# Paired-head scores, reordered buffers and engine choices, and 120 identity products in the head of an attention and soft-MoE kernel

## The chip, the cores and the metric

The kernel runs on one core of one Trainium2 chip. The metric is the device time of one execution in microseconds (us), lower is better. Engines: TensorE (PE; PEld is its weight load), VectorE (DVE), ScalarE (ACT), GpSimd (POOL), and SyncE (SP), whose queue issues the DMAs.

## The reference

Three layers follow one another, all in float32. Pooled attention over 8 batches x 8 heads x 576 queries of 64: keys and values are averaged over groups of 8, so each head has 72 of them. Then a dense layer with a rational activation, then a soft mixture of experts with 32 slots.

```python
k_p = k.reshape(B, H, 72, 8, 64).mean(axis=3);  v_p = likewise
attn = softmax(q @ k_p.T / 8);  x = attn @ v_p            # -> x [4608, 512]
h = x @ w_in                                              # [4608, 2048]
P = a0 + a1*h + a2*h**2 + a3*h**3
Q = 1 + |b0|*|h| + |b1|*h**2
x = (P / (Q + 1e-6)) @ w_out                              # [4608, 512]
logits = x @ phi                                          # [4608, 32]
slots = softmax(logits, over tokens).T @ x                # [32, 512]
out_e = relu(slots_e @ w1[e]) @ w2[e]                     # 8 experts, 4 slots each
y = softmax(logits, over slots) @ out                     # [4608, 512]
```

## The kernel before, in words

The 4608 tokens are 36 tiles of 128; four tiles make one of nine runs (r = 0 to 8).

*Head.* K and V of a batch are loaded and summed over the pool (`pooling`, line 323 on: VectorE L330 and L337, or a three-step tree on POOL, L318 to L321). For a tile, `attention` does: scores (PE L364) into two PSUM buffers `sc`, one for even and one for odd heads; maximum and subtraction (DVE L370, L374); exponential (ACT L379); sums and reciprocal (DVE L382, L383); normalization (POOL L389); two transposes (PE L398, ACT L401); the value product (PE L409); and the split into `xh` (ACT L413) and `xl` (DVE L414). The scores of a head take 64 rows: heads 2p and 2p+1 lie on partitions 0 to 63 and 64 to 127 of `q` and `kp`, and each has its own product of 72 columns.

*Weights.* `words` decodes one 128x512 block of `w_in` or `w_out` from 64-bit floats (ACT L427; DVE L428, L430, L432). There are 16 blocks of each. For `w_in`, `win` makes a high and a low part `wh` (ACT L441, POOL L442). For `w_out`, `wout` stores the block to DRAM, transposes it (PE L454) and multiplies it with `phi` (PE L463).

*Runs.* `dense(r, p)` handles one of 8 pairs of `w_in` blocks for the run: 24 products of 512 columns (L484, L485, L486) into a PSUM buffer `h` of 2 x 512, of which there are two; square, affine step and absolute value on ACT (L495, L497, L498); a multiply on POOL (L499); an affine step on DVE (L502); an affine step on POOL (L505); a multiply on POOL (L507); logarithm and exponential on ACT (L510, L513); three steps on DVE (L514, L516, L518); then logits (PE L530), transposes (PE L534) and their copy into `gt` (ACT L543). In run 0 the planner may give L499 and L507 to DVE and L505 to ACT. `routing(r)` ends a run: a running softmax over tokens, and the product `pss` (PE L593) that adds the run to `Sacc`. The attention of run r+1 lies inside run r.

*Tail.* `experts` loads 8 tiles of saved `w_out` and 64 expert tiles of 512 KB each (L628, L634), all from SP's queue in a fixed list, into buffers that come free. `tail` multiplies `Sacc` by `w_out` (PE L654), spreads the slots (L663), runs the two expert layers (PE L708, then PE L737 into `lo2`), finishes the softmax over slots of `cTs` (DVE L750 to L758, PE L765, ACT L768), and then writes the output in 18 steps of 256 tokens: two products into one `h` buffer (PE L788), the first half scaled and copied by ACT (L791), the second by DVE (L793), one store (L795).

*Order.* Nothing is issued in the order of the text. Each step is a task with an engine, a duration from a small table, a key (due time), its tiles, and perhaps alternatives on other engines. `Plan.run` simulates the engines once, on the host, and always takes the task that can start first, ties by key; this fixes each engine's instruction order, the engine of a task with alternatives, and which buffer of a pool a tile gets. At run time each engine executes its list in order. `HEAD`, `FIRST` and `RUN` (30, 105 and 75 us) are the planned lengths of the head, of run 0 and of each later run and set the keys; `LAT` and `SLACK` are the assumed delays from one engine to another and to PE.

```python
k = (round(s, 3), t.key, s + d, t.idx)
if best is None or k < best[0]:
    best = (k, t, i, s)
```

PSUM has eight banks of 512: `h` 2 x 2, `r` 1, `wk` 2, `lg` 1.

Of the kernel before, what the change touches and what calls it, by code (L numbers as in the profile page):

```python
# [18 lines left out]
SP = 72  # L19
# [11 lines left out]

HEAD, FIRST, RUN = 30.0, 105.0, 75.0
# [6 lines left out]
LAT, SLACK = 0.12, 0.6  # L39
# [64 lines left out]
class Task:  # L104
    __slots__ = ("alts", "key", "deps", "outs", "bufs", "n", "end", "start", "idx", "nbytes", "ready", "kind")


class Plan:
# [46 lines left out]
    def run(self):  # L155
# [14 lines left out]
        while left:  # L170
# [66 lines left out]
def soft_moe_kernel(ctx: ExitStack, tc: tile.TileContext, qT, kT, vP, w_in, w_out, ab, phi, w1, w2, sel, pick, out):  # L237
# [11 lines left out]
    for tag, n, w in (("q", 3, 512), ("kv", 3, 1152), ("att", 1, 1024), ("st", 4, 24), ("x", 4, 2048), ("A", 3, 1024),  # L249
                      ("S", 2, 1024), ("U", 3, 1024), ("w", 16, 1024), ("gt", 10, 1024), ("L", 1, 256), ("en", 1, 128), ("m", 3, 4),  # L250
                      ("t", 2, 512), ("wo", 1, 512)):
# [20 lines left out]
    kp = [fixed([128, 4, SP], f"kp{i}", np_=2) for i in range(2)]  # L272
# [12 lines left out]
    den = fixed([128, 1], "den")  # L285
    lgb = buf("lg", [128, 2, 130], "lg", np_=2)
# [7 lines left out]
    op("POOL", 1.0, lambda: make_identity(nc, ident), [], [idb], -100)  # L294
    op("POOL", 0.2, lambda: g_.memset(cc.t, QC), [], [cc], -90)
# [5 lines left out]
    run_len = lambda r: FIRST if r == 0 else RUN  # L301

# [3 lines left out]
    def att_key(t):  # L306
# [3 lines left out]
        if r == 1:  # L310
            return HEAD + 25 + 21.0 * j
# [11 lines left out]
    def pooling(b):  # L323
        need = att_key(first_tile[b])
        for i in range(2):
# [3 lines left out]
            o = kp[b % 2]  # L329
            op("DVE", 1.35, lambda t=t, o=o, i=i: v_.tensor_reduce(out=o.t[:, 2 * i : 2 * i + 2, :], in_=t.t, axis=AX.X, op=ALU.add),  # L330
               [], [t, (o, i)], key, alt=[("POOL", 2.8, lambda t=t, o=o, i=i: tree(t.t, o.t[:, 2 * i : 2 * i + 2, :]), True)] if b != 1 else ())
        for i in range(4):
# [5 lines left out]
               [], [t, (o, i)], key, alt=[("POOL", 2.5, lambda t=t, o=o, i=i: tree(t.t, o.t[:, 128 * i : 128 * i + 128]), True)] if b != 1 else ())  # L338
# [3 lines left out]
    def attention(t):  # L342
# [10 lines left out]
        dma_in(q, lambda: q.t, qT[t], k0 - 30, 128 * 512 * 4)  # L353
# [12 lines left out]
        op("PE", 0.6 * len(sp_), scores, [q] + [kp[x % 2] for x in batches], sc, k0, also=[st, e])  # L366
# [501 lines left out]
```

## Time and profile before

| what | value |
|---|---|
| median of 3 runs | 908.6 us (904.78 to 910.22) |
| the profiled execution | 908.17 us, span 906.4 us |
| mean granted TensorE clock | 0.946 |
| busy: PE, DVE, ACT, POOL | 91%, 69%, 67%, 58% of the span |
| moved by DMA | 97.6 MB, 108 GB/s over the span |

The span runs from the first to the last instruction; the execution's time lies 1.8 us above it. Times in the rows are microseconds from the start of the span unless marked ns. A row of the timeline gives start, length, engine, line, operation, output<-inputs, shapes and count, and in brackets how long the engine had been idle and what released it. Products overlap in TensorE, so their lengths add up to more than the time they take; the distance between their starts is the time that each one costs.

### The profile page before, as it was taken

How to read it: one execution, taken by the hardware profiler on the slowest of the kernel's cores; microseconds unless marked ns; L12 is line 12 of the kernel's file. 1: busy time of each engine (PE TensorE's matmuls, PEld its weight loads, DVE VectorE, ACT ScalarE, POOL GpSimd, SP SyncE). 2: the span in 40 equal slices, each digit the busy share in tenths (PEclk: the TensorE clock that was granted, in tenths of full speed). 3: DMA queues.
4: the chain of work that ended last, by engine and by line, in shares of the span. 5: the costliest groups of instructions: out<-in, count | busy, mean ns of one | idle time of the engine just before them, and what ended most of it. 6: DMA issues, size and time to landing. Idle time of an engine off the chain costs nothing.

```text
span 906.4 us, 15125 instructions
## 1 busy us (share of the span) xinstructions
PE 823.0 (91%) x5950; PEld 582.0 (64%) x5950; DVE 622.7 (69%) x978; ACT 605.9 (67%) x908; POOL 523.5 (58%) x333
## 2 busy tenths in 40 slices
PE   3778859799999999999999999999999999679987
PEld 3567637676777677677677767767777776433321
DVE  5888898946777777867887777758677667631023
ACT  2558757747888787788777868878877787731023
POOL 3225242856777778668866958667676766800000
PEclk9999869789999999999999999999999999869975
DMA  9694332240012100200130111000000443749947
GB/s 315 252 331 130 125 121 96 77 126 13 25 39 71 33 25 27 91 25 13 39 102 12 39 51 56 25 1 25 1 2 1 135 144 107 232 166 357 417 183 278
DMA packets 34151, 97.60 MB, mean 108 GB/s; under 512 B 3872, under 2 KB 4128, under 8 KB 34080
## 3 DMA queue, kind: packets, MB, share of 16 engines
q1 hardware_dynamic: 34080, 96.63, 31.1%
q8 instruction: 47, 0.77, 0.3%
q14 instruction: 24, 0.20, 0.1%
HBM read 82.99 MB, written 13.63 MB: 107 GB/s over the span
## 4 chain that ended last, share of the span: by engine, by line
PE 74%; DVE 12%; ACT 8%; DMA 2%; issue 2%; POOL 1%; SPq 0%; DVEq 0%; ACTq 0%; POOLq 0%
PE h L484 14%; PE h L486 13%; PE h L485 13%; PE gp L534 7%; PE av L409 4%; PE pss L593 4%; PE lg L530 4%; PE pt L398 3%; PE lo L737 3%; PE sc L364 3%; PE po L788 2%; DVE a L502 2%; PE l L708 2%; DVE r L516 2%; DVE u L514 1%
## 5 line engine op out<-in xcount | busy, mean ns | idle before, releaser
L484 PE MATMUL h<-xh,wh 128*128 128x512 f32 x576 | 249.5, 433 | 16.9 <-DVE a L502 8.6
L499 POOL TENSOR_TENSOR a<-a,s 128x1024 f32<-128x1024 f32 (+1 forms) x69 | 163.4, 2369 | 123.3 <-ACT a L497 112.9
L486 PE MATMUL h<-xh,wh 128*128 128x512 f32 x576 | 232.1, 403 | 0.5 <-POOL wh L442 0.3
L485 PE MATMUL h<-xl,wh 128*128 128x512 f32 x576 | 231.3, 402 | 0.0
L514 DVE SCALAR_TENSOR_TENSOR u<-u,r 128x512 f32<-128x512 f32 x144 | 98.2, 682 | 109.0 <-ACT r L513 105.3
L507 POOL TENSOR_TENSOR u<-u,s 128x1024 f32<-128x1024 f32 (+1 forms) x70 | 165.0, 2358 | 6.4 <-ACT s L504 1.2
L484 PEld LDWEIGHTS h<-xh,wh 128*128 128x128 f32 x576 | 111.4, 193 | 45.2 <-DVE a L502 12.3
L486 PEld LDWEIGHTS h<-xh,wh 128*128 128x128 f32 x576 | 111.0, 193 | 28.3 <-POOL wh L442 2.2
L485 PEld LDWEIGHTS h<-xl,wh 128*128 128x128 f32 x576 | 112.0, 195 | 18.1
L543 ACT ACTIVATE gt<-gp 128x512 f32<-128x512 f32 x143 | 79.8, 597 | 49.4 <-PE gp L534 47.9
L516 DVE SCALAR_TENSOR_TENSOR r<-a,abt,r 128x512 f32<-128x512 f32 x144 | 107.9, 749 | 0.0
L502 DVE SCALAR_TENSOR_TENSOR a<-h,abt,a 128x1024 f32<-128x1024 f32 (+1 forms) x73 | 92.2, 1264 | 20.1 <-POOL a L499 19.9
L518 DVE SCALAR_TENSOR_TENSOR a<-u,r 128x512 f32<-128x512 f32 x144 | 98.5, 684 | 4.3
L513 ACT ACTIVATE r<-s 128x512 f32<-128x512 f32 x144 | 86.8, 603 | 20.7 <-DVE a L518 19.8
L505 POOL TENSOR_SCALAR s<-u,gb 128x1024 f32<-128x1024 f32 (+1 forms) x71 | 84.4, 1188 | 16.3 <-DVE a L499 9.8
L498 ACT ACTIVATE u<-h 128x1024 f32<-128x1024 f32 (+1 forms) x73 | 73.7, 1011 | 26.1 <-PE h L486 25.7
L510 ACT ACTIVATE s<-u,cc 128x1024 f32<-128x1024 f32 (+1 forms) x73 | 83.2, 1140 | 6.9 <-POOL u L507 6.7
L497 ACT ACTIVATE a<-h,abt 128x1024 f32<-128x1024 f32 (+1 forms) x73 | 87.3, 1195 | 0.0
L534 PE MATMUL gp<-ident,a 128*128 128x128 f32 x576 | 84.0, 285 | 1.9 <-ACT cTs L587 1.1
L495 ACT ACTIVATE s<-h 128x1024 f32<-128x1024 f32 (+1 forms) x73 | 73.5, 1009 | 17.8 <-PE h L486 17.7
L534 PEld LDWEIGHTS gp<-ident,a 128*128 128x128 f32 x576 | 63.6, 143 | 22.0 <-issue 16.8
L389 POOL TENSOR_TENSOR at<-at,st 128x576 f32<-128x576 f32 x35 | 41.1, 1176 | 33.3 <-DVE st L383 29.7
(123 smaller groups left out, 1060.8 us busy)
## 6 DMA issues: line engine op xcount, KB each, us to landing
wx<-in_w SPq DMA_DIRECT2D x64, 512.0 KB
kst<-in_kT SPq DMA_DIRECT2D x16, 576.0 KB
qt<-in_qT SPq DMA_DIRECT2D x36, 256.0 KB
vst<-in_vP SPq DMA_DIRECT2D x32, 288.0 KB
out_dram<-o SPq DMA_DIRECT2D x18, 512.0 KB
raw<-in_w_in SPq DMA_DIRECT2D x16, 512.0 KB
raw<-in_w_out SPq DMA_DIRECT2D x16, 512.0 KB
wod<-wo SPq DMA_DIRECT2D x16, 256.0 KB
```

What stands on the lines that cost most here:

```text
L484: p_.matmul(o, w[:, 0, k], xh[r].t[:, k], start=(k == 0), stop=False)
L485: p_.matmul(o, w[:, 0, k], xl[r].t[:, k], start=False, stop=False)
L486: p_.matmul(o, w[:, 1, k], xh[r].t[:, k], start=False, stop=(k == 3))
L497: op("ACT", t_act(n, 1, 2), lambda fl=fl: a_.activation(out=fl(A), in_=fl(h), func=AF.Identity, scale=a3, bias=a2), [pt_(h), abt], [pt_(A) ...
L499: mul = lambda eng, fl=fl: eng.tensor_tensor(out=fl(A), in0=fl(A), in1=fl(S_), op=ALU.mult)
L502: op("DVE", t_dve(n, 1), lambda fl=fl: v_.scalar_tensor_tensor(out=fl(A), in0=fl(h), scalar=a1, in1=fl(A), op0=ALU.mult, op1=ALU.add), [pt ...
L507: mul = lambda eng, fl=fl: eng.tensor_tensor(out=fl(U), in0=fl(U), in1=fl(S_), op=ALU.mult)
L513: op("ACT", t_act(512, 0), lambda f=f, q=q: a_.activation(out=q.t, in_=S_.t[:, f], func=AF.Exp, scale=-1.0), [(S_, f)], [q], c + 10)
L514: op("DVE", t_dve(512), lambda f=f, q=q: v_.scalar_tensor_tensor(out=U.t[:, f], in0=U.t[:, f], scalar=QC, in1=q.t, op0=ALU.add, op1=ALU.mult),
L516: op("DVE", t_dve(512, 1), lambda f=f, q=q: v_.scalar_tensor_tensor(out=q.t, in0=A.t[:, f], scalar=a0, in1=q.t, op0=ALU.add, op1=ALU.mult) ...
L518: op("DVE", t_dve(512), lambda f=f, q=q: v_.scalar_tensor_tensor(out=A.t[:, f], in0=U.t[:, f], scalar=-2.0, in1=q.t, op0=ALU.add, op1=ALU. ...
L534: p_.transpose(pt.t[:, j, f, :], A.t[:, f, o : o + 128], ident)
```

## The change

The diff changes seven things.

1. Scores of two heads become one product. `kp` grows to 2 x 72 columns per pair of heads, zero but for two blocks; ACT copies the pooled keys into the blocks. A tile has four products of 128 rows and 144 columns. Heads are now grouped by pair in `sc` and after it.
2. The queries of the first four tiles get keys ahead of the values' loads, and 120 products of the identity with itself, which nothing reads, get the last key (1e6), so the planner puts one wherever TensorE would be idle in its plan, until they are used up. They hold the `lg` buffer until then.
3. The constants of the plan: `HEAD` 27.6, `FIRST` 105.03, keys of run 1's attention, a dense block 1.40 in place of 1.37, `SLACK` 0.86, and no delay for a buffer that was never used.
4. Engine choices (`E0`, `EITHER`, `AD`, `GD`): in run 0 POOL keeps both multiplies (L499, L507); in run 8 the last four pairs may use DVE or ACT for them and for L505, L497 may go to DVE, and the copy of the last two pairs to DVE.
5. In run 8 the last two pairs are handled in halves (before: the last one), and `r` may also use `wk` from pair 4 on.
6. Expert tiles 28 and 29 go into `q` and `at` buffers as halves, and later ones may also use `kv` and `att`. The transposed `w_out` block uses `att` or `gt`; its own buffer is gone.
7. The softmax over slots is normalized in `cTs` by DVE. In the output loop every second step uses an `h` buffer that one engine copies whole (1024 columns, ACT or DVE), the others use two banks of `wk` and `r`, each copied by ACT or DVE.

```diff
-HEAD, FIRST, RUN = 30.0, 105.0, 75.0
+HEAD, FIRST, RUN = 27.6, 105.03, 75.0
+FINE, EITHER = 2, 4
+RW, GD, AD = 4, 6, 0
+A1, A1S = 26.91, 19.0
+FILL = 120
+E0 = 12
-LAT, SLACK = 0.12, 0.6
+LAT, SLACK = 0.12, 0.86
...
-                        s0 = max(s0, c[0] + LAT)
+                        s0 = max(s0, c[0] + LAT if c[0] else 0.0)
...
-    kp = [fixed([128, 4, SP], f"kp{i}", np_=2) for i in range(2)]
+    kp = [fixed([128, 4, 2 * SP], f"kp{i}", np_=2) for i in range(2)]
...
+    idle = buf("lg", [128, 128], "idle")
...
+    for _ in range(FILL):
+        op("PE", 0.22, lambda: p_.matmul(idle.t, ident, ident, start=True, stop=True), [idb], [idle], 1e6)
...
+    for i in range(2):
+        op("POOL", 0.75, lambda i=i: g_.memset(kp[i].t, 0.0), [], [kp[i]], -94)
...
-            return HEAD + 25 + 21.0 * j
+            return HEAD + A1 + A1S * j
...
+            for par in range(2):
+                rr = slice(64 * par, 64 * par + 64)
+                op("ACT", 0.33, lambda o=o, i=i, par=par, rr=rr: a_.activation(out=kp[b % 2].t[rr, 2 * i : 2 * i + 2, SP * par : SP * par + SP], in_=o.t[rr], func=AF.Copy),
+                   [o], [(kp[b % 2], i)], key + 0.1)
...
-        dma_in(q, lambda: q.t, qT[t], k0 - 30, 128 * 512 * 4)
+        dma_in(q, lambda: q.t, qT[t], (k0 if t > 3 else -8.2 + 0.1 * t) - 30, 128 * 512 * 4)
...
-                    for par in range(2):
-                        rr = slice(64 * par, 64 * par + 64)
-                        p_.matmul(sc[par].t[t0:t1, SP * p : SP * p + SP], q.t[rr, p, t0:t1], kp[bb % 2].t[rr, p, :], start=True, stop=True)
+                    p_.matmul(sc[p // 2].t[t0:t1, 2 * SP * (p % 2) : 2 * SP * (p % 2) + 2 * SP], q.t[:, p, t0:t1], kp[bb % 2].t[:, p, :], start=True, stop=True)
...
-        subs = [(0, 1), (1, 2)] if r == NR - 1 and p == NPAIR - 1 else [(0, 2)]
+        subs = [(0, 1), (1, 2)] if r == NR - 1 and p >= NPAIR - FINE else [(0, 2)]
+        either = r == 0 or r == NR - 1 and p >= EITHER
...
-               alt=[("DVE", t_dve(n), lambda mul=mul: mul(v_), True)] if r == 0 else ())
+               alt=[("DVE", t_dve(n), lambda mul=mul: mul(v_), True)] if (E0 & 1 if r == 0 else either) else ())
...
-            q = buf("r", [128, 512], "r")
+            q = buf(["r", "wk"] if r == NR - 1 and p >= RW else "r", [128, 512], "r")
...
+            if 28 <= n < 30:
+                halves = [buf("q", [128, 512], "wx"), buf("q" if n == 28 else "at", [128, 512], "wx")]
...
-                b = buf(["kv", "att"] if n < 8 else ["w", "gt", "A"], [128, 2, 512], "wx")
+                b = buf(["kv", "att"] if n < 8 else ["w", "gt", "A", "kv", "att"], [128, 2, 512], "wx")
...
+            op("DVE", t_dve(n), lambda c3=c3, cm=cm, nt=nt: v_.tensor_tensor(out=c3(), in0=c3(), in1=cm(2).rearrange("p (a o) -> p a o", o=1).to_broadcast([128, nt, 32]), op=ALU.mult),
+               [csum], [cr], kk, port=True)
...
-            po = buf("h", [128, 2, 512], "po", np_=2)
+            po = [buf("h", [128, 2, DM], "po")] if n % 2 == 0 else [buf(["wk", "r"], [128, DM], "po") for _ in range(2)]
...
+            for i in range(len(po)):
+                w = 2 * DM // len(po)
+                oo = lambda i=i, o=o, po=po: o.t if len(po) == 1 else o.t[:, i]
+                op("ACT", t_act(w), lambda i=i, oo=oo, po=po: a_.activation(out=oo(), in_=po[i].t, func=AF.Copy), [po[i]], [o if len(po) == 1 else (o, i)], kk,
+                   alt=[("DVE", t_dve(w), lambda i=i, oo=oo, po=po: v_.tensor_copy(oo(), po[i].t), False)])
```

## Rows read from the trace of the kernel before

**Rows 1.** The page, part 1: busy us, share of the span, instructions.

```profile
PE 823.0 (91%) x5950; PEld 582.0 (64%) x5950; DVE 622.7 (69%) x978; ACT 605.9 (67%) x908; POOL 523.5 (58%) x333
```

**Rows 2.** Stretches: length, busy us of each engine (instructions), granted clock, DMA share, GB/s.

```profile
6.00:55.00 49.00, 30.21 (x204) 23.34 (x205) 41.14 (x71) 20.54 (x34) 15.82 (x15) 1.00 0.87 306
55.00:219.00 164.00, 142.76 (x943) 111.75 (x942) 129.02 (x195) 108.68 (x173) 81.21 (x61) 0.86 0.37 121
219.00:749.00 530.00, 519.99 (x4076) 388.23 (x4079) 394.43 (x624) 417.89 (x609) 390.84 (x228) 1.00 0.14 42
781.00:806.00 25.00, 12.34 (x104) 7.42 (x102) 16.19 (x26) 15.07 (x30) 12.93 (x10) 0.64 0.66 220
806.00:820.00 14.00, 11.83 (x87) 4.90 (x87) 3.11 (x10) 2.50 (x6) 0.29 (x1) 0.90 0.70 269
...
868.00:907.00 39.00, 28.35 (x74) 8.46 (x74) 13.85 (x19) 12.71 (x20) 0.00 (x0) 0.57 0.64 243
```

**Rows 3.** The timeline of TensorE, the head.

```profile
8.20 1.99 PE L364 MATMUL sc<-kp,qt 64*128 64x72 f32 x16 [8.20 <-DMA qt<-in_qT]
14.28 2.10 PE L364 MATMUL sc<-kp,qt 64*128 64x72 f32 x16 [4.09 <-DMA qt<-in_qT]
...
42.43 1.23 PE L364 MATMUL sc<-kp,qt 64*64 64x72 f32 x30 [0.25 <-ACT a L401]
49.62 1.98 PE L409 MATMUL av<-a,vp 72*64 72x128 f32 x16 [5.96 <-DVE at L374]
...
55.06 0.77 PE L484 MATMUL h<-xh,wh 128*128 128x512 f32 x1
...
57.34 0.59 PE L486 MATMUL h<-xh,wh 128*128 128x512 f32 x1
57.76 0.40 PE L484 MATMUL h<-xh,wh 128*128 128x512 f32 x1
57.99 0.39 PE L485 MATMUL h<-xl,wh 128*128 128x512 f32 x1
```

**Rows 4.** The chain that ended last: start, us, what; ends of run 0 and run 7.

```profile
219.12 3.57 PE pss L593 x32
...
748.57 3.57 PE pss L593 x32
```

**Rows 5.** The timeline of TensorE at the scores of a tile in run 1.

```profile
241.03 1.12 PE L364 MATMUL sc<-kp,qt 64*128 64x72 f32 x16
242.07 0.50 PE L484 MATMUL h<-xh,wh 128*128 128x512 f32 x1
```

**Rows 6.** The timeline of POOL in the drain.

```profile
780.67 2.39 POOL L499 TENSOR_TENSOR a<-a,s 128x1024 f32<-128x1024 f32 x1 [3.34 <-ACT s L495]
...
791.62 2.50 POOL L507 TENSOR_TENSOR u<-u,s 128x512 f32<-128x512 f32 x2
```

**Rows 7.** Groups of the whole span: count | busy us, mean ns | idle before.

```profile
L587 ACT ACTIVATE cTs<-ptr 128x128 f32<-128x128 f32 x9 | 2.5, 277 | 0.0
```

**Rows 8.** The timeline of TensorE, one pair's transposes in run 8.

```profile
765.50 1.09 PE L534 MATMUL gp<-ident,a 128*128 128x128 f32 x8
```

**Rows 9.** Groups of VectorE from 55 to 220 us.

```profile
L499 DVE TENSOR_TENSOR a<-a,s 128x1024 f32<-128x1024 f32 x4 | 5.0, 1249 | 5.6 <-ACT a L497 5.6
...
L507 DVE TENSOR_TENSOR u<-u,s 128x1024 f32<-128x1024 f32 x3 | 3.7, 1219 | 0.0
```

**Rows 10.** Stretches of the expert weights, columns as in rows 2.

```profile
810.00:864.00 54.00, 51.02 (x330) 18.75 (x323) 4.75 (x9) 4.68 (x9) 0.29 (x1) 1.00 0.96 379
850.00:860.00 10.00, 10.00 (x33) 2.86 (x32) 0.00 (x0) 0.00 (x0) 0.00 (x0) 1.00 1.03 419
```

**Rows 11.** The output loop: TensorE's timeline, then VectorE's group from 868 us on.

```profile
894.17 3.34 PE L788 MATMUL po<-so,cTs 32*128 32x512 f32 x8 [0.31 <-DVE o L793]
897.82 2.48 PE L788 MATMUL po<-so,cTs 32*128 32x512 f32 x6 [0.31 <-DVE o L793]
...
L793 DVE TENSOR_SCALAR o<-po,csum 128x512 f32<-128x512 f32 x18 | 13.4, 750 | 19.1 <-ACT o L791 19.1
```

More of the change, by code (lines that the diff above doesn't have):

```diff
@@ L104 @@
 class Task:
-    __slots__ = ("alts", "key", "deps", "outs", "bufs", "n", "end", "start", "idx", "nbytes", "ready", "kind")
+    __slots__ = ("alts", "key", "deps", "outs", "bufs", "n", "end", "start", "idx", "nbytes", "ready", "kind", "name")
 class Plan:
@@ L328, in pooling @@
             dma_in(t, lambda t=t: t.t, kT[b, i], key - 30, 128 * 2 * SP * 32)
[L329 to L331 removed]
+            o = buf("ks", [128, 2, SP], "ks")
+            op("DVE", 1.35, lambda t=t, o=o: v_.tensor_reduce(out=o.t, in_=t.t, axis=AX.X, op=ALU.add),
+               [], [t, o], key, alt=[("POOL", 2.8, lambda t=t, o=o: tree(t.t, o.t), True)] if b > 1 or b == 0 and E0 & 8 else ())
+            for par in range(2):
+                rr = slice(64 * par, 64 * par + 64)
+                op("ACT", 0.33, lambda o=o, i=i, par=par, rr=rr: a_.activation(out=kp[b % 2].t[rr, 2 * i : 2 * i + 2, SP * par : SP * par + SP], in_=o.t[rr], func=AF.Copy),
+                   [o], [(kp[b % 2], i)], key + 0.1)
         for i in range(4):
@@ L337, in pooling @@
             op("DVE", 1.2, lambda t=t, o=o, i=i: v_.tensor_reduce(out=o.t[:, 128 * i : 128 * i + 128], in_=t.t, axis=AX.X, op=ALU.add),
-               [], [t, (o, i)], key, alt=[("POOL", 2.5, lambda t=t, o=o, i=i: tree(t.t, o.t[:, 128 * i : 128 * i + 128]), True)] if b != 1 else ())
+               [], [t, (o, i)], key, alt=[("POOL", 2.5, lambda t=t, o=o, i=i: tree(t.t, o.t[:, 128 * i : 128 * i + 128]), True)] if b > 1 or b == 0 and E0 & 8 else ())
     xh, xl = {}, {}
@@ L361, in scores @@
                 for t0, t1, bb in sp_:
-                    for par in range(2):
-                        rr = slice(64 * par, 64 * par + 64)
-                        p_.matmul(sc[par].t[t0:t1, SP * p : SP * p + SP], q.t[rr, p, t0:t1], kp[bb % 2].t[rr, p, :], start=True, stop=True)
-        op("PE", 0.6 * len(sp_), scores, [q] + [kp[x % 2] for x in batches], sc, k0, also=[st, e])
+                    p_.matmul(sc[p // 2].t[t0:t1, 2 * SP * (p % 2) : 2 * SP * (p % 2) + 2 * SP], q.t[:, p, t0:t1], kp[bb % 2].t[:, p, :], start=True, stop=True)
+        op("PE", 1.0 + 0.2 * (len(sp_) - 1), scores, [q] + [kp[x % 2] for x in batches], sc, k0, also=[st, e])
         v3 = lambda par: sc[par].t[:, 0 : 4 * SP].rearrange("p (h s) -> p h s", s=SP)
@@ L486, in g1 @@
                         p_.matmul(o, w[:, 1, k], xh[r].t[:, k], start=False, stop=(k == 3))
-                seq("g1", op("PE", 1.37, g1, [wh[2 * p + f], xh[r], xl[r]], [(h, f)], c - step + f * step / 2, after=was("g1"), kind="g"))
+                seq("g1", op("PE", 1.40, g1, [wh[2 * p + f], xh[r], xl[r]], [(h, f)], c - step + f * step / 2, after=was("g1"), kind="g"))
         A, S_, U = (buf(x, [128, 2, 512], x.lower(), np_=2) for x in "ASU")
-        subs = [(0, 1), (1, 2)] if r == NR - 1 and p == NPAIR - 1 else [(0, 2)]
+        subs = [(0, 1), (1, 2)] if r == NR - 1 and p >= NPAIR - FINE else [(0, 2)]
+        either = r == 0 or r == NR - 1 and p >= EITHER
         for f0, f1 in subs:
@@ L496, in dense @@
             seq("sq", P.tasks[-1])
-            op("ACT", t_act(n, 1, 2), lambda fl=fl: a_.activation(out=fl(A), in_=fl(h), func=AF.Identity, scale=a3, bias=a2), [pt_(h), abt], [pt_(A)], c)
+            op("ACT", t_act(n, 1, 2), lambda fl=fl: a_.activation(out=fl(A), in_=fl(h), func=AF.Identity, scale=a3, bias=a2), [pt_(h), abt], [pt_(A)], c,
+               alt=[("DVE", t_dve(n, 1), lambda fl=fl: v_.tensor_scalar(out=fl(A), in0=fl(h), scalar1=a3, scalar2=a2, op0=ALU.mult, op1=ALU.add), False)] if r == NR - 1 and p >= AD else ())
             op("ACT", t_act(n), lambda fl=fl: a_.activation(out=fl(U), in_=fl(h), func=AF.Abs), [pt_(h)], [pt_(U)], c)
@@ L615, in experts @@
             key += 0.01
+            if 28 <= n < 30:
+                halves = [buf("q", [128, 512], "wx"), buf("q" if n == 28 else "at", [128, 512], "wx")]
+                w, e, k = it
+                v = lambda b: b.t if len(b.t.shape) == 2 else b.t.rearrange("p a h s -> p (a h s)")[:, 0:512]
+                for h, b in enumerate(halves):
+                    src = (w1 if w == 1 else w2)[e, k][:, 512 * h : 512 * h + 512]
+                    op("SP", 0.06, lambda b=b, src=src, v=v: nc.sync.dma_start(out=v(b), in_=src), [], [b], key, nbytes=128 * 2048)
+                ew[it] = (halves, lambda h, halves=halves, v=v: v(halves[h]))
+                continue
             if n < 4 or 24 <= n < 28:
@@ L632, in experts @@
                 o = lambda b=b, at=at: at(b)
-                ew[it] = ((b, part), o)
+                ew[it] = ([(b, part)], lambda h, o=o: o()[:, h])
                 op("SP", 0.06, lambda o=o, src=src: nc.sync.dma_start(out=o(), in_=src), [], [(b, part)], key, nbytes=128 * 4096)
```

31 lines of the change are left out of this document (14 added, 17 removed).

## The prediction

> **What bounds the kernel now.** I read the page first: TensorE busy 91% of the span, VectorE 69% [rows 1]. Busy shares hide stages, so the stretches come next [rows 2]. The reader should see five of them.
>
> - From 6 to 55 us TensorE is busy 30.2 of 49 us, VectorE 41.1. Nothing is close to its limit, so this is a chain. In the order of TensorE [rows 3] the first scores start at 8.20, the second tile's wait 4.09 us for its queries, the fourth tile's value product waits 5.96 us for VectorE, and the first dense product is at 55.06. Equal dense products stand 0.42 us apart there and 0.23 us apart from 57.76 on, 2.7 us into back-to-back work: the spacing goes from that of 1.2 GHz to that of 2.4, although the clock column says 1.00 for the whole stretch.
> - From 55 to 219 us (run 0, ended by its routing product at 219.12, [rows 4]) VectorE is busy 129 of 164 us, because it also decodes the weights; TensorE 143, part of it at half clock (granted 0.86).
> - From 219 to 749 us, seven runs take (748.57 - 219.12)/7 = 75.6 us each with TensorE busy 520 of 530 us. That is bound by TensorE; all waiting there is 10 us.
> - From the last dense product to the last routing product (781 to 806) TensorE is idle half the time: the last pairs drain through POOL, VectorE and ScalarE.
> - From 806 on DMA bounds the expert weights, and the output loop follows from 870.
>
> **The change part by part.**
>
> *Paired scores.* Per tile, eight 64-row products of 72 columns become four 128-row ones of 144; each fp32 product is two instructions. Before: 16 instructions from 241.03 to the next product at 242.07, 0.065 us each for 72 columns [rows 5]. Twice the columns at twice the time, half as many: 1.04 us again, 0 over the 36 tiles. Bounds: 0.041 us per instruction, as in the form with 64x64 blocks [rows 3], is 0.7 us and thus 0.4 us gained per tile, -13 us; the same 0.4 us lost is +13. I take 0, from the row of the same row count.
> The Trainium skill, "TensorE: Matmul & The Clock Gate", Part 3, says that products of few rows in different row groups run side by side; by it the change undoes a packing that was worth half of the old 1.04 us, and the sum would be 36 x 0.5 = 18 us worse. The spacing of 0.065 us in the old one-batch form shows no such overlap.
> The zero padding is two memsets of 128x576 on POOL. They stand in the 8.2 us in which TensorE waits for its first data [rows 3], and even at the 2.4 us of a POOL pass over 128x1024 [rows 6] both end by then; 0. Placing the two halves costs ScalarE 32 copies of about 0.28 us [rows 7], 9 us over the kernel; ScalarE is busy 418 of 530 us in the steady part, which hides them; in the head the last two sit in front of the first scores: +0.6 us.
>
> *Query order and the 120 products.* All four query tiles now precede the values in SP's queue. The second scores lose their wait: 4.09 us, of which about 2 are due anyway, since the two score buffers of the first tile come free only after their VectorE steps (I put half of the wait down to these). The values land some 2 us later; nothing shown waits for them in that part. The filler products: one 128x128 fp32 product is two instructions. At full clock eight such instructions took 1.09 us [rows 8], so at most 0.27 us a product; at half clock I scale that by the dense products, 0.42/0.23 [rows 3], to 0.50. For 120 that is 33 or 60 us. TensorE is idle 19 of the 49 us [rows 2] and all of the 6 before, and at full clock its own 30 us shrink to 15, leaving 40. The products start when the identity is ready (an estimate: 1.4 us, after two short POOL steps); if the clock rises as it did at 57.76, some 3 us go at half speed, and 33 + 3 + 15 = 51 fits into 55 and they stand in idle time. What they can cost is queue position: TensorE executes in order, so scores that become ready early stand behind them. What they bring: the eight scores, transposes and value products per tile at 2.4 GHz. Scores took 1.99 us in the head against 1.04, so about 3 us per tile with the others, on a chain that passes two PSUM buffers in turn. Four tiles: -12 us at best for the chain. But VectorE must still decode all weights; what it wins is its idle time before 55 us, at most 8 us (49 us of window, 41.1 busy, [rows 2]). Bounds: -8 and, at half clock, +36 (below). I take -4, half of that idle time.
>
> *Run 0.* The multiplies may no longer go to VectorE: 4 + 3 of them, 5.0 + 3.7 = 8.7 us [rows 9], move to POOL at 2.39 us each, 16.7 us [rows 6]; POOL is busy 81 of 164 us, so there is room. VectorE, busy 129 of 164 us, has the most to lose there after TensorE, so I credit 8.7 us, less 1.7 for the longer latency: -7. Bounds: 0 if run 0 is held by the chain through POOL, -20 if the half-clock stretches go too. If the longer POOL chain is fully exposed: +8 (7 x 1.14). New keys for run 1's attention only reorder.
>
> *Runs 1 to 7.* No work removed. A longer assumed latency can save part of 10 us of waits: -1, between +3 and -6.
>
> *Drain.* POOL does the multiplies of the last pairs in series, one starting at 780.67 and the last two halves from 791.62 to 794.12 [rows 6], 13 us after the last dense product; VectorE's steps and the transposes follow. With halves for the last two pairs, and VectorE or ScalarE allowed to take multiplies and affine steps, VectorE's 1.25 us (or about 0.7 per half) replaces 2.4. VectorE is idle 8.8 of 25 us there, ScalarE 10. Moving three POOL multiplies of 2.4 saves about 7 us of POOL's queue and adds 3.7 to VectorE: I take -5, between -2 and -8. Next in line is the three-step VectorE chain per half.
>
> *Expert weights.* From 810 to 864 DMA moved 20.5 MB; at the 419 GB/s of 850 to 860 that is 49 us of 54 [rows 10]. The products of the second layer cannot end before the last tile, so the transfer bounds 867. Two tiles of 0.52 MB now go early into query and attention buffers: -2.5 us. Four more buffers, free when the products of the linear layer end, can fill part of the other 5 us, in which it waited for buffers: I credit 2. Together -4.5, between -2 and -7. The earlier drain shifts this transfer by its own 5 us, since the buffers it waits for are freed by the last routing product.
>
> *Output.* Each of 18 steps is a product, a ScalarE copy, then a VectorE copy; VectorE waits 19.1 us for ScalarE in total, and one buffer's circle (product, copy, copy) takes 3.65 us for every second step: TensorE's rows of the same buffers stand 3.65 us apart [rows 11]. The clock fell to a granted mean of 0.57 there while TensorE waited [rows 2]. With one reader per buffer and 7 banks in place of 4, two steps cost VectorE at most 2 x 0.75 us [rows 11] for its halves, while ScalarE takes the 1024-wide one: under 0.8 us a step. Then DMA bounds: 18 x 0.524 = 9.44 MB at 380 GB/s (243 at a share of 0.64 over the stretch, [rows 2]) is 24.8 us. With an estimated 2.5 us ahead of the first store (one product, one wide copy) and as much after the last one, the loop takes 29.8 us from 870, where it took 36.4: -6.5, between -4 and -9. The normalization moves into three VectorE steps; like the subtractions beside them they lie between 806 and 820, where all of VectorE's work is 3.1 of 14 us [rows 2]: 0.
>
> Sum: -4 + 0.6 - 7 - 1 - 5 - 4.5 - 6.5 = -27.4. The profiled execution took 908.2 us (span 906.4), 0.4 below the median of 908.6. So 880.8, I say **881**.
>
> **The rivals.**
>
> 1. *Run 0 keeps its time.* VectorE's gain is used up by POOL's longer chain, and what the head wins is waited out at the weights. For it: TensorE is busy 143 of run 0's 164 us too. Against: VectorE is the fullest engine there. Only steady part, drain, weights and output are left: -17, so 891.
> 2. *Run 0 gains more.* Better packed, TensorE keeps 2.4 GHz: the granted 0.86 over 164 us with 143 busy means about 20 us lost to half clock. Getting most of it: 881 - 18 = 863.
> 3. *The products block the head (slower).* If the clock falls back between them because each real step still waits for data, 60 us of products plus 30 of work end at 91 instead of 55: +36. Run 0 has 164 - 143 = 21 us of idle to catch up; with half of it +26, and less the tail's 16 about 918; without catching up 928. It decides from the point at which the head and run 0 lose over 16 us, the tail's sum. Against: in [rows 3] it rose 2.7 us into dense work.
> 4. *Pairing costs TensorE time.* A loss of 0.5 us for each of 36 tiles in a part bound by TensorE: 881 + 18 = 899. For it: the 0.041 us spacing of one form; against: 0.065 in the form used by 32 tiles.
> 5. *The order gets worse.* The planner's order is new everywhere, and its table gives run 0 105 us where the trace has 164: 15 to 25 us lost somewhere in runs 0 to 7: 896 to 906.
>
> **How the numbers follow.** Forecast 0.45, rival 1 0.22, rival 2 0.17, rival 3 0.05, rival 4 0.04, rival 5 0.07. A measurement of this kernel tells about 1%, 9 us. Faster by over 1% (below 899.5): the forecast, rivals 1 and 2, and a good third of 4 and 5: 0.88. Within 1%: the rest of 4 and 5: 0.07. Slower: 0.05. The range takes in the forecast, rival 1 with its spread, and most of rival 2: 862 to 898.
>
> **What would show it.** Right: scores at about 1 us per tile with 8 instructions; filler products at 0.21 to 0.27 us apart from some 4 us on; first dense product at 45 to 52; first routing product at 205 to 212; 75 to 76 us per run after it; last dense to last routing product 19 to 21 us instead of 25; two weight tiles before the gap; output loop of 27 to 30 us with DMA share near 1 and no ScalarE-to-VectorE wait in it. Wrong: filler products at 0.43 us or more all along, a first dense product after 60, run 0 ending after 219, or an output loop that still takes 34 us.

## The result, and the profile after

The changed kernel takes 877.2 us (median of 4 runs, 875.8 to 882.4) where the kernel before takes 906.7 beside it (904.4 to 910.2): a ratio of 0.968, interval 0.963 to 0.974. Forecast were 881 us and a range of 862 to 898. The profiled execution took 878.2 us, its span 876.4. The total is right; run 0's term and the pairing's are not, and their errors cancel in part.

The kernel after, the page, part 1 (columns as in [rows 1]):

```profile
PE 810.1 (92%) x5870; PEld 597.6 (68%) x5870; DVE 622.6 (71%) x976; ACT 613.3 (70%) x941; POOL 534.5 (61%) x336
```

VectorE is as busy as before to a tenth of a microsecond. So the 30 us are not work taken from it. Next the stretches of the kernel after, in the columns of [rows 2]; the borders follow its own stages, which end earlier:

```profile
6.00:48.00 42.00, 40.09 (x375) 38.24 (x375) 34.94 (x62) 20.64 (x40) 13.26 (x13) 1.00 0.95 332
48.00:211.00 163.00, 139.18 (x899) 111.37 (x899) 135.26 (x204) 118.14 (x190) 91.57 (x55) 0.91 0.40 128
211.00:736.00 525.00, 517.13 (x3852) 392.13 (x3850) 395.44 (x625) 418.88 (x625) 396.94 (x237) 1.00 0.14 44
768.00:788.00 20.00, 11.36 (x87) 6.80 (x90) 12.85 (x24) 11.39 (x24) 7.76 (x7) 0.67 0.69 264
788.00:844.00 56.00, 53.34 (x359) 19.09 (x355) 6.25 (x15) 5.28 (x11) 0.29 (x1) 0.96 0.87 347
844.00:877.00 33.00, 13.79 (x74) 3.91 (x74) 6.65 (x10) 14.49 (x20) 0.00 (x0) 0.75 0.76 286
```

From 6 to 48 us TensorE is now busy 40 of 42 us, but much of that is filler. VectorE's 34.9 of 42 and DMA's share of 0.95 (0.87 from 6 to 55 us in [rows 2]) are the ones that do work. The chain that ended last has the routing products, whose starts in [rows 4] were 219.12 and 748.57:

```profile
211.29 3.60 PE pss L609 x32
...
736.37 3.57 PE pss L609 x32
787.84 5.79 PE pss L609 x32
```

With the first dense product (48.22, shown below; 55.06 in [rows 3]) and the first output product (846.52; 870.18 before) these give the table. Before, run 8's routing product started at 806.00.

| stage | before | after | difference |
|---|---|---|---|
| start to first dense product | 55.06 | 48.22 | -6.8 |
| to the routing product of run 0 | 164.06 | 163.07 | -1.0 |
| runs 1 to 7 | 529.45 | 525.08 | -4.4 |
| run 8, with the drain | 57.43 | 51.47 | -6.0 |
| routing to first output product | 64.2 | 58.7 | -5.5 |
| output loop | 36.2 | 29.9 | -6.3 |
| sum | 906.4 | 876.4 | -30.0 |

The head, TensorE's timeline of the kernel after (columns as in [rows 3]):

```profile
1.36 10.31 PE L303 MATMUL idle<-ident 128*128 128x128 f32 x66 [1.36 <-POOL at L307]
11.51 1.15 PE L378 MATMUL sc<-kp,qt 128*128 128x144 f32 x8
...
44.81 1.09 PE L423 MATMUL av<-a,vp 72*64 72x128 f32 x16 [1.23 <-DVE at L388]
48.22 0.77 PE L498 MATMUL h<-xh,wh 128*128 128x512 f32 x1
...
51.36 0.41 PE L499 MATMUL h<-xl,wh 128*128 128x512 f32 x1
51.60 0.39 PE L500 MATMUL h<-xh,wh 128*128 128x512 f32 x1
```

Three things are to be seen. The first row is 33 products in one piece (a product is two instructions); the scores behind them start at 11.51, though ScalarE has placed the second half of their keys by 8.53: it starts that copy at 7.88 and takes 0.65. The waits of 4.09 us for the queries and of 5.96 us for VectorE [rows 3] are gone, the latter down to 1.23. And the dense products still begin at half speed: 0.24 us apart only from 51.36 on, 3.1 us into them. The granted clock of 48 to 51 us, 0.50, says it too:

```profile
48.00:51.00 3.00, 3.00 (x10) 2.42 (x10) 2.93 (x6) 1.54 (x4) 1.30 (x1) 0.50 0.63 178
```

The output loop of the kernel after, groups of the stretch from 840 us on, against 19.1 us in which VectorE waited for ScalarE [rows 11]:

```profile
L822 ACT ACTIVATE o<-po 128x1024 f32<-128x1024 f32 (+1 forms) x18 | 13.7, 808 | 4.8 <-PE po L816 4.8
L823 DVE COPY o<-po 128x512 f32<-128x512 f32 x9 | 6.2, 692 | 10.2 <-PE po L816 10.2
```

Both readers now wait for TensorE alone.

### The profile page after: what moved, and what is told of

The parts are those of the page before. It is cut to its first block, busy times and chain, and to the rows that moved or that the text cites. A ratio compares the mean times of both kernels' runs of the same rounds, so it can differ in the third digit from the quotient of the medians.

```text
span 876.4 us, 15025 instructions
## 1 busy us (share of the span) xinstructions
PE 810.1 (92%) x5870; PEld 597.6 (68%) x5870; DVE 622.6 (71%) x976; ACT 613.3 (70%) x941; POOL 534.5 (61%) x336
## 4 chain that ended last, share of the span: by engine, by line
PE 76%; DVE 9%; ACT 8%; issue 2%; POOL 2%; DMA 1%; SPq 0%; ACTq 0%; DVEq 0%; POOLq 0%
PE h L498 14%; PE h L500 13%; PE h L499 13%; PE gp L550 7%; PE pss L609 4%; PE av L423 4%; PE lg L546 4%; PE idle L303 3%; PE pt L412 3%; PE sc L378 3%; PE lo L762 3%; DVE a L518 2%; PE l L733 2%; PE po L816 1%; DVE r L532 1%
## 5 line engine op out<-in xcount | busy, mean ns | idle before, releaser
L515 POOL TENSOR_TENSOR a<-a,s 128x1024 f32<-128x1024 f32 (+1 forms) x73 | 171.7, 2352 | 127.1 <-ACT a L512 105.1
L499 PE MATMUL h<-xl,wh 128*128 128x512 f32 x576 | 230.8, 401 | 0.0
L523 POOL TENSOR_TENSOR u<-u,s 128x1024 f32<-128x1024 f32 (+1 forms) x74 | 173.0, 2339 | 7.9 <-ACT s L520 2.6
L499 PEld LDWEIGHTS h<-xl,wh 128*128 128x128 f32 x576 | 111.4, 193 | 17.9
L518 DVE SCALAR_TENSOR_TENSOR a<-h,abt,a 128x1024 f32<-128x1024 f32 (+1 forms) x74 | 92.3, 1247 | 8.3 <-POOL a L515 7.5
L521 POOL TENSOR_SCALAR s<-u,gb 128x1024 f32<-128x1024 f32 (+1 forms) x67 | 79.4, 1186 | 9.6 <-DVE a L515 2.9
L512 ACT ACTIVATE a<-h,abt 128x1024 f32<-128x1024 f32 (+1 forms) x66 | 78.8, 1193 | 0.0
```

Source lines behind the costliest of these rows:

```text
L499: p_.matmul(o, w[:, 0, k], xl[r].t[:, k], start=False, stop=False)
L515: mul = lambda eng, fl=fl: eng.tensor_tensor(out=fl(A), in0=fl(A), in1=fl(S_), op=ALU.mult)
L518: op("DVE", t_dve(n, 1), lambda fl=fl: v_.scalar_tensor_tensor(out=fl(A), in0=fl(h), scalar=a1, in1=fl(A), op0=ALU.mult, op1=ALU.add), [pt ...
L523: mul = lambda eng, fl=fl: eng.tensor_tensor(out=fl(U), in0=fl(U), in1=fl(S_), op=ALU.mult)
```

## The experiments

Each is the changed kernel with one edit, unless said. Executions of the same kernel spread by up to 8.5 us, so stages are compared as well as medians.

**The products not issued.** The 120 tasks stay in the plan, so every other instruction keeps its place, but nothing is executed for them.

```diff
-op("PE", 0.22, lambda: p_.matmul(idle.t, ident, ident, start=True, stop=True), [idb], [idle], 1e6)
+op("PE", 0.22, lambda: None, [idb], [idle], 1e6)
```

> The 120 identity products stay in the plan, so that every engine keeps its order, but are not issued. Theory A (they earn the earlier dense start by raising TensorE's clock in the head): scores back to about 2 us per tile, first dense product at 53 to 56 us instead of 48.2, the whole 5 to 8 us longer, 882 to 885. Theory B (the earlier start comes from the query order and the new order alone, and the products only stand in front of the first scores): first scores at 8.6 instead of 11.5, first dense product at 45 to 48, the whole 873 to 877.

880.4 us (875.3 to 883.8), ratio 0.971 (0.967 to 0.976). TensorE's timeline of this run:

```profile
6.81 1.30 PE L378 MATMUL sc<-kp,qt 128*128 128x144 f32 x4 [6.81 <-ACT kp L346]
...
43.11 1.98 PE L423 MATMUL av<-a,vp 72*64 72x128 f32 x16 [1.72 <-DVE at L388]
...
48.55 0.77 PE L498 MATMUL h<-xh,wh 128*128 128x512 f32 x1
```

and its stretch of the head:

```profile
6.00:48.00 42.00, 27.77 (x154) 21.49 (x154) 35.33 (x63) 21.19 (x41) 13.32 (x13) 0.73 0.92 333
```

The first half of the scores starts 4.7 us earlier (the second at 8.80), TensorE has a granted clock of 0.73 in place of 1.00, and the first dense product is at 48.55 in place of 48.22. What stays equal is VectorE's work (35.3 us) and the rate of the loads (333 GB/s).

The equal end of the head hides two differences. One is when VectorE comes to its fourth sum of a value block (L353), first in the kernel after, then in this run:

```profile
38.12 1.22 DVE L353 TENSOR_REDUCE vp<-vst 72x128 f32<-72x1024 f32 x1 [0.40 <-DMA vst<-in_vP]
```

```profile
36.61 1.22 DVE L353 TENSOR_REDUCE vp<-vst 72x128 f32<-72x1024 f32 x1 [0.58 <-DMA vst<-in_vP]
```

It is 1.5 us earlier here, and the last value product before the dense part follows it (43.11 against 44.81). The other is the clock: from this value product to the first dense product it is 5.4 us here, at a granted clock of 0.50 (1.2 GHz), and 3.4 us in the kernel after, at 0.96. So the clock is worth 2.0 us in this place, and the earlier sum made up for it.

**The first 24 products priced at half clock,** so that the plan puts fewer of them ahead of the scores.

```diff
-for _ in range(FILL):
-    op("PE", 0.22, ...
+for i in range(FILL):
+    op("PE", 0.34 if i < 24 else 0.22, ...
```

> The plan prices the first 24 products at 0.34 us instead of 0.22, so 22 instead of 33 stand in front of the first scores; the other engines keep their order. If the 3 us that the first scores wait behind products are on the path to the first dense product: first scores at about 8.6, first dense product 2 to 3 us earlier, 874 to 875. If the head is set by what comes after (value loads, VectorE, the two score buffers): first scores earlier, the rest as it was, 877.

878.5 us (875.0 to 880.2). The scores start at 8.83, 2.7 us earlier; the first dense product is at 48.42. The delay of the first scores costs nothing that shows: VectorE, now earlier too, waits 1.93 us for the load of its fourth sum and starts it at 38.37. Of the products 14 now stand at 41.82, behind the last scores (one in the changed kernel), and the dense products begin at full speed here (0.33 us apart, then 0.23); run 0 is not shorter for it (165.2 us).

**200 products.**

```diff
-FILL = 120
+FILL = 200
```

> 200 products in place of 120, so that the plan fills TensorE past 43 us, where the products end and the clock falls before the dense part. If the clock at the dense start matters: first dense products at full clock, about 1.5 us gained, 875 to 876. If the products cost their place in TensorE's queue: each of the 80 more takes 0.18 us and up to 14 us are lost, 880 to 891.

885.8 us (884.3 to 888.8), some 7 us above the run before, on the same chip. TensorE's timeline:

```profile
43.24 3.39 PE L303 MATMUL idle<-ident 128*128 128x128 f32 x28
...
50.95 0.48 PE L498 MATMUL h<-xh,wh 128*128 128x512 f32 x1
51.26 0.39 PE L499 MATMUL h<-xl,wh 128*128 128x512 f32 x1
```

The dense products begin at full speed (0.31 us apart; 0.42 and more in the changed kernel), as they did in the run before, and start 2.5 us later than there; run 0's routing product is at 217.46. Of the 5.9 us between the two profiles 2.5 lie in the head, 1.3 in run 0 and 2.6 in runs 1 to 7. The missing warm start was not the loss. A product takes 0.22 us at the full clock in the kernel after (18 of them 4.01 us from 15.93 on), where 0.18 was expected.

**Run 0's multiplies free again to go to VectorE.**

```diff
-E0 = 12
+E0 = 15
```

> In run 0 VectorE may take the multiplies again, as before the change. By the step of the prediction (VectorE is what run 0 waits for, 8.7 us of multiplies cost 7 us): run 0 gets 5 to 7 us longer, 882 to 884. By the rival read from the trace after (VectorE's total up to the end of run 0 did not change, because value reductions took the place of the multiplies): run 0 within 3 us of 163, the whole within 4 us of 877.

885.2 us (884.1 to 887.3): 4.8 above the first run and 6.7 above the second, all on one chip, with no overlap of the runs. VectorE has the multiplies again (4 at L515, 3 at L523, 9.1 us). By these medians the step is worth some 5 to 7 us. The profile does not put them where they were forecast: run 0 takes 167.2 us, against 166.5 and 165.2 in the first two runs, and the head ends 1.7 and 1.8 us later than theirs. VectorE's total to the end of run 0 is 175.8 us here, against 171.5 and 171.4, so the choice by itself does relieve VectorE. But in the change as a whole that total did not fall: 170.5 us in 219 before, 171.6 in 211 after. Two groups of VectorE tell why, first the kernel before, from 0 to 219 us:

```profile
L337 DVE TENSOR_REDUCE vp<-vst 72x128 f32<-72x1024 f32 x8 | 9.6, 1205 | 3.5 <-DMA vst<-in_vP 3.5
L428 DVE TENSOR_SCALAR wi<-wi 128x512 int32<-128x512 int32 x16 | 6.7, 419 | 0.0
```

and the kernel after, from 0 to 211:

```profile
L353 DVE TENSOR_REDUCE vp<-vst 72x128 f32<-72x1024 f32 x13 | 15.6, 1207 | 2.9 <-DMA vst<-in_vP 2.9
L442 DVE TENSOR_SCALAR wi<-wi 128x512 int32<-128x512 int32 x16 | 9.7, 606 | 0.1
```

Five sums of values came over from POOL, 6.0 us. The 16 decode steps of this group take 606 ns on average instead of 419, 3.0 us more, but all decode steps together (L442, L444 and L446; L428, L430 and L432 before) only 66.1 us instead of 64.6, since another group became shorter.

**Scores unpaired, everything else changed.** The keys stay in the wide buffer; eight products of 64 rows and 72 columns read its blocks, and the value product takes the heads in the old order.

```diff
-p_.matmul(sc[p // 2].t[t0:t1, ...], q.t[:, p, t0:t1], kp[bb % 2].t[:, p, :], ...)
+for par in range(2):
+    rr = slice(64 * par, 64 * par + 64)
+    p_.matmul(sc[par].t[t0:t1, SP*p : SP*p + SP], q.t[rr, p, t0:t1], kp[bb % 2].t[rr, p, SP*par : SP*par + SP], ...)
```

> Scores as before the change (eight products of 64 rows and 72 columns per tile, even and odd heads in two PSUM buffers), on the new key layout and in the new order. The prediction's step: nothing gained or lost by the pairing on TensorE, 877 within 2 us, runs 1 to 7 at 75.3 us each. The rival that pairing undoes a useful overlap: each run 2 us shorter here (0.5 us for each of 4 tiles), 859 to 863. If the pairing saves weight loads: each run 0.3 to 1 us longer here, 879 to 885.

889.0 us (886.1 to 891.9). Runs 1 to 7 take 744.62 - 216.18 = 528.4 us, 3.3 more. TensorE's timeline of a tile, unpaired:

```profile
305.77 1.12 PE L380 MATMUL sc<-kp,qt 64*128 64x72 f32 x16
306.81 0.50 PE L500 MATMUL h<-xh,wh 128*128 128x512 f32 x1
```

and the kernel after:

```profile
300.89 1.14 PE L378 MATMUL sc<-kp,qt 128*128 128x144 f32 x8
301.77 0.49 PE L498 MATMUL h<-xh,wh 128*128 128x512 f32 x1
```

From the first score to the next product it is 1.04 us unpaired, as in [rows 5], and 0.88 paired; most other tiles of one batch in runs 1 to 7 show the same two numbers. The rest of the distance to 877 arose in head and run 0 (216.2 against 211.3) and is not put down to the pairing.

**The old output loop.** One buffer for both readers, ScalarE for the first half, VectorE for the second, without the scale.

```diff
-po = [buf("h", [128, 2, DM], "po")] if n % 2 == 0 else [buf(["wk", "r"], [128, DM], "po") for _ in range(2)]
+po = buf("h", [128, 2, 512], "po", np_=2)
...
+op("ACT", 0.69, ..., [(po, 0)], [(o, 0)], kk)
+op("DVE", 0.75, ..., [(po, 1)], [(o, 1)], kk)
```

> The output loop as before (one buffer of two banks, first half copied by ScalarE, second by VectorE), the normalization in the slot softmax kept. The prediction's step: the loop is 6.5 us longer, 883.5, with VectorE waiting for ScalarE about 19 us in total and one buffer's circle at 3.65 us again. If the gain of the tail came from the weights alone: 877 to 879.

889.4 us (884.9 to 892.4). The loop takes 888.6 - 853.74 = 34.9 us against 29.9: 5.0 of the difference. Waits of VectorE from 850 us on (us in total, times, longest):

```profile
DVE o L819 <- ACT o L818: 18.6, 9, 2.2
```

TensorE's timeline, first here, then in the kernel after; eight instructions are two steps:

```profile
872.83 2.67 PE L815 MATMUL po<-so,cTs 32*128 32x512 f32 x8 [0.82 <-DVE o L819]
876.33 2.67 PE L815 MATMUL po<-so,cTs 32*128 32x512 f32 x8 [0.83 <-DVE o L819]
```

```profile
855.51 1.14 PE L816 MATMUL po<-so,cTs 32*128 32x512 f32 x8 [0.67 <-ACT o L822]
857.32 1.14 PE L816 MATMUL po<-so,cTs 32*128 32x512 f32 x8 [0.67 <-ACT o L822]
```

Two steps take 3.50 us with the old loop and 1.81 with the new one.

**The old drain** (last pair alone in halves, and the choices of run 8 taken back).

```diff
-FINE, EITHER = 2, 4
-RW, GD, AD = 4, 6, 0
+FINE, EITHER = 1, 8
+RW, GD, AD = 8, 7, 8
```

> Run 8 as before: halves for the last pair only, the multiplies and the affine steps fixed to POOL and ScalarE, one buffer for the exponential. The prediction's step: from the last dense product to the last routing product 25 us again instead of 20 or so, 5 us longer in all, 882. If the weights' transfer bounds the tail whatever the drain does: the drain longer, but the end of the second expert layer within 1 us of 843.7 and the whole at 877 to 878.

887.6 us (887.4 to 888.5). The chain that ended last in this run:

```profile
740.74 3.57 PE pss L609 x32
798.30 5.14 PE pss L609 x32
```

Run 8 takes 57.6 us against 51.5: 6.1. POOL's last multiplies end at 785.9 (783.39 and 2.49); in the kernel after they end at 777.2, in a run 8 that began 4.4 us earlier. So POOL is done 4.3 us sooner by the new choices. From the last routing product to the end it is 87.7 us here and 88.6 in the kernel after, so the transfer of the weights did not take up the loss. The edit takes back all of the drain's parts at once; what each is worth was not measured.

**The old buffers of the expert tiles.**

```diff
-if 28 <= n < 30:
+if False:
...
-b = buf(["kv", "att"] if n < 8 else ["w", "gt", "A", "kv", "att"], [128, 2, 512], "wx")
+b = buf(["kv", "att"] if n < 8 else ["w", "gt", "A"], [128, 2, 512], "wx")
```

> No expert tiles in the query and attention buffers, none of the later ones in the key and value buffers. The prediction's step: the transfer that bounds the second expert layer is 4.5 us longer, 881.5, with a dip in the DMA rate after the linear layer. If the transfer has slack now: 877 to 878.

886.6 us (881.5 to 887.4). From the last routing product to the end it is 93.8 us against 88.6, with the two early tiles and the further buffers both taken back. A stretch of 10 us soon after that product, first this run, then the kernel after (columns as in [rows 2]):

```profile
800.00:810.00 10.00, 8.98 (x80) 3.61 (x84) 0.23 (x1) 0.82 (x2) 0.00 (x0) 1.00 0.74 284
```

```profile
798.00:808.00 10.00, 8.95 (x86) 3.54 (x80) 0.23 (x1) 0.82 (x2) 0.00 (x0) 1.00 1.03 418
```

**The changed kernel and the one without products again, side by side,** because head and run 0 had come out unlike from run to run.

> The changed kernel itself, beside the three others. Head and run 0 of one and the same order ended between 211 and 219 us in the runs so far, runs 1 to 7 took 524 to 525 us in all of them: so 877 to 884, with the spread in the head and run 0 alone.

> The 120 products planned but not issued, again, with more rounds and beside the changed kernel. If the products earn what their faster clock suggests: 3 to 8 us longer than the changed kernel beside it. If the head waits for VectorE's list of decode steps and not for TensorE (first dense product at 48.55 against 48.22 us before): within 2 us of it, either way.

883.4 us (880.0 to 885.8) with the products, 880.4 (878.9 to 884.2) without: ratios of 0.973 (0.970 to 0.976) and 0.971 (0.968 to 0.974). They can't be told apart, and if one leads it is the one without. The changed kernel's profile here has the first dense product at 54.17 and run 0's routing product at 217.09. Its head:

```profile
6.00:48.00 42.00, 37.30 (x348) 35.66 (x347) 30.32 (x55) 17.77 (x34) 12.82 (x13) 0.99 0.97 312
```

The same program, loads as dense (0.97), but 312 GB/s instead of 332, and VectorE has done 4.6 us less. Its fourth sum of values, which started at 38.12 in the first profile of the kernel after, and the last value product:

```profile
42.23 1.22 DVE L353 TENSOR_REDUCE vp<-vst 72x128 f32<-72x1024 f32 x1 [3.11 <-DMA vst<-in_vP]
```

```profile
48.74 1.97 PE L423 MATMUL av<-a,vp 72*64 72x128 f32 x16 [3.02 <-DVE at L388]
```

VectorE waits 3.11 us for the load, the value product comes 3.9 us later, and from it to the first dense product it is 5.4 us, at a granted clock of 0.50: TensorE had waited 3.02 us just before. Without the products the fourth sum starts at 38.04 and the first dense product at 49.98, also 5.4 us behind its value product. Runs 1 to 7 took 524.8 us with the products; the 524 to 525 us named above hold for the runs so far but the one of 200 products and the unpaired one (527.9 and 528.4).

**All sums in run 0 free to go to POOL,** to give VectorE back the 6 us.

```diff
-... if b > 1 or b == 0 and E0 & 8 else ())
+... if True else ())
```

> POOL may also take the key and value sums of batch 1, which lie in run 0 and were VectorE's alone. If VectorE's time is what run 0 waits for: up to six sums of 1.2 us off VectorE, run 0 4 to 7 us shorter, 870 to 874 where the changed kernel gives 877. If POOL's tree (2.3 us and the shared decode steps it slows) costs as much: no gain, or 1 to 4 us longer.

880.8 us (877.6 to 885.0) beside the 883.4 above: not separable. The first dense product came at 57.0 and run 0's routing product at 213.66. So run 0 itself took 156.7 us, the shortest of all profiles and, as forecast, 6.3 us under the changed kernel's beside it, but its head was the longest.

**The kernel before with the new output loop alone** (and the normalization in `cTs`).

> The kernel before with the new output loop and normalization alone. By the prediction's step 6.5 us less than before, 900; by what undoing it in the changed kernel showed, 5 us less, 901. If the old order hides it: within 2 us of before. Its head and run 0 are those of before: first dense product at 55, first routing product at 219.

900.8 us (900.0 to 903.6), ratio 0.993 (0.991 to 0.996) to 906.9: the loop alone brings 6.1 us. In the profile it is 94.1 us from the last routing product to the end, 100.4 before. Its order of the head is the old one, with the first dense product at 55.90, but run 0's routing product came at 214.92 where 219 was expected; that head:

```profile
6.00:48.00 42.00, 25.50 (x176) 19.33 (x176) 33.59 (x58) 16.87 (x28) 13.26 (x13) 1.00 0.86 295
```

## Why the prediction was right, and where it was not

**Output (-6.5).** Right. -6.3 in the profile, 5.0 lost when undone, 6.1 won when done alone. The mechanism is the forecast one: the wait of VectorE for ScalarE is gone, and DMA bounds the loop (its share is 1.02 from 855 to 875 us; TensorE's last step starts at 862.74, the stores go on to 876). The new loop has one reader per buffer and also seven banks where four were; no run separates the two.

**Expert weights (-4.5).** Right: -5.5, and 5.2 when undone. The gain lies where the buffers were missing, in the first 20 us after routing. The two early tiles (2.5) and the further buffers (2) were not measured apart.

**Drain (-5).** Right: -6.0, and 6.1 when undone. From the last dense product (769.02) to the last routing product it is 18.8 us, where 19 to 21 were forecast.

**Pairing (0).** Too small. The failed step is "twice the columns at twice the time": 144 columns took 0.110 us an instruction and 72 took 0.065, so eight are 0.88 us and sixteen 1.04. A tile of one batch gains 0.16 us, and 22 of them lie in runs 1 to 7: 3.5 us. The three tiles of two batches there gain nothing (1.14 us for 16 instructions, against 0.98 for 32 in one of them). Undoing the pairing cost 3.3 us in runs 1 to 7, which agrees. Rival 4 is out.

**Runs 1 to 7 (-1).** -4.4 in the profile; less the 3.3 of the pairing, -1.1 is left for the order. The Trainium skill ("TensorE: Matmul & The Clock Gate", Part 3) lets products in different row groups run side by side, which would have made unpaired scores the cheaper form; at 0.065 us each, unpaired here and before, no such overlap is seen. In the tiles of two batches, whose products have 64 output rows, an instruction takes 0.031 us, about half; whether that is overlap or a shorter weight load no run separates.

**Query order and products (-4).** The order did what was said: the 4.09 us wait is gone, DMA's share rose, and the first dense product came at 48 to 51 in nine of the ten profiles of the new order (without the run of 200 products and that of the free sums), at 55 and 56 in the two of the old. The products gave less. The step that failed is "eight scores, transposes and value products at 2.4 GHz ... half of that idle time": they did run at 2.4 GHz, but that chain does not set when the last value product of the head starts. VectorE's list does: in those ten profiles, with the products or without, this value product starts 6.5 to 7.2 us after VectorE's fourth sum of values. And the sum waits for its load, for nothing in the run with the old drain and for 3.11 us in the second profile of the changed kernel. So "nothing shown waits for them in that part", said of the values, failed too. In the kernel before, the third and the fourth sum did not wait; the fourth started at 43.72, 5.6 us later than in the kernel after.

What the clock does bring lies at the end of the head, 2.0 us from the last value product to the first dense one. In one pair of profiles an earlier sum made up for them; in the pair on another chip the clock had fallen in both, and the 4.2 us by which the head ended earlier without the products are those of the sum. The medians show nothing of it. Between the two profiles of the changed kernel the loads ran at 332 and at 312 GB/s from 6 to 48 us; why the rate differs between executions of the same program was not settled. The rate was lower still in the old order (302 and 295), but the third and fourth sum did not wait for loads there, so the rate is not what separates the two orders. The warning "scores that become ready early stand behind them" came true with 3 us, and cost nothing that shows: without it VectorE waited for the load instead.

**Run 0 (-7).** The undo costs 5 to 7 us by the medians of one chip, of which its profile shows 0.7 to 2.0 in run 0. The reason fails for the change as a whole: VectorE was not relieved. What the multiplies freed (8.7 us) was refilled by five sums (6.0), one more affine step (L518, 1.2) and longer decode steps (1.5), and POOL's busy time in run 0 rose from 81 to 92 us. In the profile run 0 kept its time (-1.0), as rival 1 said; head and run 0 together gave -7.8, against -10.4 forecast. Even that is a lucky draw: in the five profiles in which head and run 0 are as the change has them, run 0's routing product stood at 211.3, 214.4, 216.4, 217.1 and 218.6, 215.6 on average; in the two of the old order at 219.1 and 214.9, 217.0 on average. So of the -10.4 about 1.4 us stand on average, over values that spread by 7.

The length of run 0 goes with TensorE's granted clock. From the first dense product to run 0's routing product (columns as in [rows 2]), first in the old order, the kernel before and the one with the new output loop alone:

```profile
55.06:219.12 164.06, 142.82 (x946) 111.76 (x950) 129.07 (x196) 108.68 (x173) 81.27 (x61) 0.86 0.37 121
55.90:214.92 159.02, 136.71 (x946) 107.17 (x950) 132.43 (x197) 108.65 (x173) 82.71 (x61) 0.91 0.39 126
```

then in the new order, the kernel after and the run with the old drain:

```profile
48.22:211.29 163.07, 139.25 (x902) 111.25 (x904) 135.33 (x204) 118.21 (x191) 91.86 (x55) 0.91 0.40 128
48.22:216.42 168.20, 144.88 (x902) 116.30 (x904) 134.02 (x203) 117.88 (x190) 90.75 (x55) 0.86 0.39 124
```

In either order 5 us lie between 0.86 and 0.91, and the -1.0 of the table compares a run 0 at 0.91 with one at 0.86. At the same clock run 0 is 4 us longer with the change, where -7 was forecast. Some of that may be work that the earlier first dense product moved from the head into run 0. Whether the clock makes run 0 longer, or waits in run 0 lower the clock, no run separates.

**The sum.** Runs 1 to 7, drain, weights and output give -22 us in the first profile and -23 in the second (from run 0's routing product to the end 665.1 and 664.5 us, 687.3 before), where the forecast had -17; head and run 0 give -1.4 on average and -7.8 at best, where it had -10.4. The medians agree: the whole was 29.5 us shorter in one comparison and 23.5 in the other, which leaves about 7 and 1 for head and run 0. The errors have opposite signs and cancel, which is why 881 lies between the measured medians of 877 and 883. No version here is clearly faster than the changed kernel; the one without the products is as fast with less in it.

**Left open.** Whether a later due time for the fourth tile's scores or the free sums without products would shorten the head was not tried. The keys of the first queries and the constants of the plan were not taken back by themselves, so which of them moved VectorE's fourth sum forward is not shown. The spread of run 0's length, 162 to 168 us over profiles with the same order, goes with the granted clock, but its cause is not shown.

## What to carry to other kernels

Before warming an idle engine, ask what ends last in that stage: here 120 products raised an engine's granted clock from 0.73 to 1.00 over 42 us, and the head ended no earlier, because its last steps start when VectorE's list, and the load in it, lets them. Moving work off an engine gains only what the planner doesn't put back on it, so look at the engine's total over the stage, not at the operation. What paid in every run here is a shared buffer with two readers in turn replaced by more buffers with one reader each, and idle buffers given to a transfer that waits for them.

## What was not expected of the hardware

Columns are not the whole price of a product: 144 columns of 128 rows took 0.110 us where 72 columns of 64 rows took 0.065, so one wide product with half its weights zero beats two narrow ones by 15%. Where the products have 64 output rows it does not (1.14 us against 0.98).

The same loads from the same queue, in the same order, ran at 312 GB/s in one execution and at 332 in another, with DMA's share near its full in both (0.97 and 0.95); VectorE's fourth sum of values waited for its load and started 4.1 us later in the slower one, and the first dense product 6 us later.

A decode step of VectorE (L442, 128x512, int32) mostly takes 0.42 us, but two of the 16 in the group above took 2.58 and 1.15 us in the kernel after, and those two are most of its higher average. They lie beside a multiply of POOL and end just after it. The longer of them and its multiply:

```profile
99.97 2.58 DVE L442 TENSOR_SCALAR wi<-wi 128x512 int32<-128x512 int32 x1
```

```profile
99.69 2.59 POOL L515 TENSOR_TENSOR a<-a,s 128x1024 f32<-128x1024 f32 x1 [1.63 <-ACT a L512]
```

The step ends at 102.55, the multiply at 102.28. All nine long decode steps up to the end of run 0 (of L442, L444 and L446) overlap an instruction of POOL; some others overlap one and keep their length, so the overlap alone is not the whole condition.
